# Last-row items: one turned by TensorE again, v's loads reordered, and softmaxes moved ahead of copies on ScalarE

## The chip, the cores and the metric

The kernel runs on one core of a Trainium2 chip. The metric is the device time of one execution in microseconds: 1477.64 before the change (median of three runs, 1477.17 to 1479.41). The engines are called PE (TensorE, matmuls; PEld are its weight loads), ACT (ScalarE), DVE (VectorE), POOL (GpSimd) and SP (SyncE, which here only issues DMAs).

## The reference

```python
# top-k attention, q, k, v: (8, 8, 576, 64) float32
scores = scale * np.matmul(q, k.transpose(0, 1, 3, 2))
kth = np.partition(scores, -top_k, axis=-1)[..., -top_k:-top_k + 1]   # top_k = 32
scores = np.where(scores >= kth, scores, -1e9)
attn = np.exp(scores - np.max(scores, axis=-1, keepdims=True))
attn = attn / (np.sum(attn, axis=-1, keepdims=True) + 1e-09)
x = np.matmul(attn, v)                 # to (4608, 512): tokens by heads * 64
# block with exact gelu
h = x @ w_in                           # (512, 2048)
g = 0.5 * h * (1.0 + erf(h / sqrt(2)))
out = g @ w_out                        # (2048, 512)
```

All arithmetic is in float32.

## The kernel before

**Items and slots.** Two heads of a batch make a pair, so a batch has 4 pairs. 576 query rows are four blocks of 128 and a rest of 64. An *item* is 128 query rows of one pair (both heads, 2 x 576 scores for each row in the tile `s`), or, for the rest, the last 64 rows of two pairs together: a *last-row item* (`items[i][1] == NM`). A batch has 16 ordinary and 2 last-row items; the last-row items stand at the end of an even batch and at the beginning of an odd one. So in each two batches (36 items, `RINGS`) four last-row items stand in a row: 16, 17, 18, 19 and then 52 to 55, 88 to 91, 124 to 127. There are N = 144 items.

The main loop (line 1174) has one *slot* n for each item. It is written out by hand and sets the order of every engine's instructions, in slot n:

- scores of item n+2 on PE (in an even slot those of n+3 too), and ACT's copies of them to `s`, scaled;
- the selection of the 32nd largest score of item n on DVE (`top_k`), with POOL's help (`sum_up`, `smaller`). Its threshold goes from POOL (`threshold`, L516, L517) to ACT;
- the softmax of item n-1 on ACT, for each of the two heads e a `select` (L536, which pushes all scores below the threshold far down) and an exponential (L548) whose sum goes to `den`. POOL adds a small number (`add_small`, L529), DVE takes the reciprocal at the end of its `top_k` (`inverse`, L523), POOL multiplies (`normalise`, L571);
- the transposition of item n-2, which brings keys to the partitions for the product with v. It goes one of two ways. By PE (`transposes`): one transpose of the ends (`tails`, tile `tp_t`, L647) and eight of the main keys (tile `tp`, L661), each followed by ACT's copy to `pt` (L650, L676). Or by DVE and DRAM, where `squared(i)` holds: DVE transposes 32 x 32 squares (`square_p`, L595, in the middle of `top_k`), SP writes the tile to DRAM (`write_p`, `turned`, L605, four DMAs), and a slot later reads it back (`read_p`, L615, four DMAs) into `pt`. Before the change these are all last-row items from 52 on and most even ordinary items;
- the product with v (`attend`, L727 for two ordinary items of a pair at once, L738 for a last-row item) and the copy of the result to `xT` (`copy_x`, L732, L744). There is one `pt` tile for two items. After a pair's last product the next batch's v is loaded into the same buffers (`load("v", ...)`, L138 and L142, four DMAs).

**The block with gelu.** Between all this PE works off a fixed list of pieces (`mlp`): `h_ps` = first product (L790), `gelus` on ACT (L806), and the second product by seven smaller products (L944, L946), whose sums POOL makes (`run_small`, up to six steps a slot). The gelu and the exponential lie in different table sets of ACT, so an odd slot, in which gelus run, has two table loads.

**Banks.** From slot 13 on the short tiles of PE's results (`o`, `t_ps`, `tp_t`, `seven`) all live in one bank with one buffer (`bank`, tag `z`): the next one can be written once ACT has copied the one before. `tp` and one of the two score tiles share the tag `pr`, `h_ps` and the other the tag `l1`.

**Last-row items from 52 on** (`delayed`): their products come later than others. Item 52's stands in slot 56 (`even_last`), those of 53 in the middle of slot 57 and of 54 and 55 in slot 59 (`mid`, `mids`). Each `mids` copies x, issues the next read (`read_p`) and one of the loads of v (`soon`); the others of these loads are kept until the slot's end (`issue`, `late_issues`, `flush`). SP takes all its DMAs in the order of the program, with a wait of one holding those behind it.

Of the kernel before, what the change touches and what calls it, by code (L numbers as in the profile page):

```python
# [14 lines left out]
def kernel(  # L15
# [78 lines left out]
            return raws[n][pair % 2 if pair < SQUARES else 0]  # L94
        return raws[n][pair % len(raws[n])]

    held, late_issues, soon = [False], [], []

    def issue_soon():
        while soon:  # L100
# [9 lines left out]
    def flush():  # L110
        held[0] = False
        while late_issues:
            late_issues.pop(0)()

    def load(n, pair, queue=None, queue2=None):
        if pair >= n_pairs:
# [161 lines left out]
    def bank(name):  # L278

        tag = "z" if few[0] else ("z", "y0", "y1", "y2")[turn[0] % 4]  # L280
        turn[0] += 1
        return ps.tile([P, 512], f32, tag=tag, bufs=1, name=name)
# [292 lines left out]
    def squared(i):  # L575

        if not SINGLE.stop - 2 < i < N - 2:
            return False
        return items[i][1] == NM or (i % 2 == 0 and i % RINGS != 12)

    def delayed(i):

# [117 lines left out]

    copies = []

    def column(tok):

        at = tok % RING
        return at if at < COLS else at - COLS

    def attend(i):

        if i < 0 or i >= N:  # L710
            return False
        pair, t = items[i]
        b, at = divmod(pair, NP)
        if t < NM and t % 2 == 0:
            return False
        pt = pt_now[0]
        o = bank("o")
        n, row = (2 * P, (t - 1) * P) if t < NM else (TL, SM)
        tok = place_of(b, row)
        gap = RING if t == NM else COLS if tok % RING >= COLS else RING - COLS  # L720
        assert read[0] >= tok - gap + n
        c = slice(column(tok), column(tok) + n)
        if t < NM:
            vt = raw_of("v", pair)
            for j in range(NJ):
                for e in range(2):
                    nc.tensor.matmul(  # L727
                        o[e * D : (e + 1) * D, 0:n], lhsT=vt[:, j, e, :],
                        rhs=pt[:, e * NJ + j if j < NM else NM, :],
                        start=(j == 0), stop=(j == NJ - 1),  # L730
                    )
            copies.append(lambda: nc.scalar.copy(out=xT[:, at, c], in_=o[:, 0:n]))  # L732
        else:
            for r in range(2):
                vt = raw_of("v", pair + r)
                for j in range(NJ):
                    for e in range(2):
                        nc.tensor.matmul(  # L738
                            o[e * D : (e + 1) * D, r * TL : (r + 1) * TL],
                            lhsT=vt[:, j, e, :],  # L740
                            rhs=pt[:, e * NJ + j if j < NM else NM, i % 2 * P :][:, half(r, e)],
                            start=(j == 0), stop=(j == NJ - 1),
                        )
            copies.append(lambda: nc.scalar.copy(  # L744
                out=xT[:, at : at + 2, c],
                in_=o[:, 0 : 2 * TL].rearrange("p (r n) -> p r n", n=TL),
            ))

        if t == (NM if b % 2 == 0 else NM - 1):
            for r in range(2 if t == NM else 1):  # L750
                f = lambda r=r: load("v", pair + r + NP)
                if r == 0 and delayed(i):
                    soon.append(f)
                else:
                    issue(f)
        if at == (NP - 1 if t < NM else NP - 2):
            assert n_tok[0] == tok
            n_tok[0] = tok + n
        return True
# [414 lines left out]
    for n in range(ahead):  # L1174

        held[0] = n < N and squared(n - 2)
        mid = [i for i in (n - 5, n - 4) if delayed(i) and n % 2 and (i % 2 or i in starts)]
        even_last = delayed(n - 4) and n % 2 == 0 and n - 4 not in starts
        if not mid and not even_last:
            read_p(n - 3)  # L1180

        def mids():
            attend(mid.pop(0))
            if not mid:
                copy_x()
                read_p(n - 3)
                issue_soon()
        left[0] = room_in(n)
        few[0] = n > START + 2
        eager[0] = n > N  # L1190
        left[0] += closes(n - 3) - closes(n - 2)
        if not waits(unit_in(n)):
            weights_add(unit_in(n))
        if n > 0:
            larger(n + 1)
        for piece in squares_in.pop(n, []):
            piece()
        if n == 1:

            for e in range(2):  # L1200
                select(0, e)
            for e in range(2):
                softmax(0, e)
        two = few[0] and n % 2 == 0 and n + 3 < N and items[n + 3][1] < NM
        scores(n + 2, two)
        if two:
            scores(n + 3)
        if even_last:
            product = attend(n - 4)
            issue_soon()  # L1210
            read_p(n - 3)
        else:
            product = not delayed(n - 3) and attend(n - 3)
        if len(mid) == 2:
            mids()
        late = n > START
        if n != 1 and n < START:

            for e in range(2):
                select(n - 1, e)  # L1220
            softmax(n - 1, 0)
        copy_x()
        if n == START:

            for e in range(2):
                select(n - 1, e)
            softmax(n - 1, 0)
        if waits(unit_in(n)):
            weights_size(unit_in(n))
            weights_add(unit_in(n))  # L1230
        mlp(1)
        if closes(n - 3):
            ready[0] = n_tok[0]
        if few[0] and n % 2:
            run_gelus()
        tr = transposes(n - 2)
        if product and n > START and done[0] < len(pieces) and pieces[done[0]][0] > ready[0]:

            for piece in tr[:1]:
                piece(n + 2 if few[0] else None)  # L1240
            tr, ready[0] = tr[1:], n_tok[0]
        if not few[0] and n > START:
            softmax(n - 1, 0)
        mlp(1)
        if n != 1 and not late:
            softmax(n - 1, 1)
        if few[0]:
            softmax(n - 1, 0)
            if n % 2:
                mlp(ODD)  # L1250
                if mid:
                    mids()
        mlp(1)
        prep = prep_in.pop(n, [])
        if n == 0:
            weights_size(unit_in(1))
            keep_busy(14, ident)
        if n == START + 1:

            for piece in prep:  # L1260
                piece(None)
            prep = []
        if len(prep) > 1 and len(tr) == 3:
            tr, prep = tr[:1] + prep[:1] + tr[1:], prep[1:]
        now = tr[:-1]
        if few[0]:
            now, tr, prep = tr + prep[:1], [], prep[1:]
        for x, piece in enumerate(now):
            piece(n + 2 if few[0] else None)
            ready[0] = n_tok[0]  # L1270
            if few[0] and x == 2:
                break
            mlp(1)
        ready[0] = n_tok[0]
        if late:
            softmax(n - 1, 1)
        if n > 0:
            smaller(n + 1)
        add_small(n - 1)
        for piece in tr[-1:] + prep:  # L1280
            piece(None)
            mlp(1)
        if n < START:

            keep_busy(4 if n == 0 else 8 if product else 14 if n < 5 else 18, ident)

        run_gelus()
        mlp(left[0])
        run_gelus()
        if n < N:  # L1290
            top_k(n, lambda: inverse(n - 1), lambda: square_p(n - 2))
            write_p(n - 2)
            flush()
            if n == 0:
                larger(1)
        else:
            inverse(n - 1)
        threshold(n)
        if n == 0:
            smaller(1)  # L1300
        normalise(n - 1)
        sum_up(n + 2)
        if n in sums_in:
            weight_sums(sums_in[n])
        run_small(6)

        if n > 0 and not waits(unit_in(n + 1)):
            weights_size(unit_in(n + 1))
        run_stores()
        if n == N:  # L1310
            run_stores()
        for m in (n + 1, n + 2):

            if m > 2 and waits(unit_in(m)) == (m == n + 1):
                load_weights(m)
        if n < NP:
            load("v", n)
        if n == 5:
            nc.vector.memset(flat["k"][0][TL:, 0:TL], 0.0)
            load("q", SQUARES)  # L1320
            load("k", SQUARES)
# [38 lines left out]
```

## Time and profile before

| | us |
|---|---|
| median of 3 runs (lowest to highest) | 1477.64 (1477.17 to 1479.41) |
| the profiled execution, its own time | 1479.29 |
| span of that execution, first to last instruction | 1477.5 |
| busy: PE | 1449.7 (98%) |
| busy: DVE | 1307.8 (89%) |
| busy: POOL | 1142.0 (77%) |
| busy: ACT | 1082.8 (73%) |
| mean granted clock of PE | 0.999 |

A row of the timeline gives the start and the duration in microseconds, the engine, the line, the operation, the written and the read tiles, shapes and a count; the brackets give the idle time of the engine before it and what ended that. PE's records are halves of a matmul: x12 are six matmuls. "SPq" rows are the issues of DMAs on SP's queue. A row of the waits names who waited, for whom, the total, how often and the longest. A row of a group gives the busy time and the mean length of one, then the idle time before.

### The profile page before, as it was taken

Reading aid. Unit: us, or ns where it says so; the run is one execution under the profiler, and the core shown is the slowest. Engines: PE = TensorE matmul, PEld = TensorE weight load, DVE = VectorE, ACT = ScalarE, POOL = GpSimd, SP = SyncE. Lnnn points to the kernel's source line nnn. Section 1 sums busy time; section 2 is a strip of 40 time slices with the busy share of each in tenths; the row PEclk is TensorE's granted clock in tenths of the full one; section 3 lists DMA queues with packets and bytes.
Section 4 is the critical chain, followed back from the end, with each engine's and each line's share of the span. In section 5 each row is a group of like instructions: output and inputs, shape, how many; then the busy total and the mean of one; then the engine's idle time right before and its main releaser. Section 6 shows DMA issues by size and latency. Waiting matters only on the chain. (4 is left out here: it accounts for less than half of the span.)

```text
span 1477.5 us, 26521 instructions
## 1 busy us (share of the span) xinstructions
PE 1449.7 (98%) x8693; PEld 1134.6 (77%) x8693; DVE 1307.8 (89%) x3331; ACT 1082.8 (73%) x1902; POOL 1142.0 (77%) x1290
## 2 busy tenths in 40 slices
PE   8999999999999998999999999999999999999999
PEld 6776677887777776888777777787777777787787
DVE  7999899999999999899999999899999999898701
ACT  7999877877777686777777777677777777677620
POOL 6877567878898888777898978787788888887632
PEclk9999999999999999999999999999999999999999
DMA  7425210045435356345534347344543435523300
GB/s 198 144 86 129 78 47 1 24 92 103 93 71 91 67 107 129 65 95 112 102 81 78 74 74 151 76 92 96 99 101 73 89 63 97 125 61 73 68 15 15
DMA packets 544713, 127.04 MB, mean 86 GB/s; under 512 B 466464, under 2 KB 536128, under 8 KB 544576
## 3 DMA queue, kind: packets, MB, share of 16 engines
q1 hardware_dynamic: 543312, 124.93, 39.8%
q8 instruction: 69, 1.13, 0.3%
q14 instruction: 68, 0.56, 0.1%
q10 hardware_dynamic: 1200, 0.39, 0.1%
q0 software_dynamic: 64, 0.03, 0.0%
HBM read 80.47 MB, written 44.83 MB: 85 GB/s over the span
## 5 line engine op out<-in xcount | busy, mean ns | idle before, releaser
L790 PE MATMUL h_ps<-xT,w_in_sb 128*128 128x256 f32 (+1 forms) x2560 | 534.1, 361 | 0.0
L790 PEld LDWEIGHTS h_ps<-xT,w_in_sb 128*128 128x128 f32 x2560 | 437.5, 190 | 73.3 <-issue 25.2
L502 DVE MAX8 top<-lists 128x8 f32<-128x576 f32 (+1 forms) x792 | 475.5, 639 | 0.0
L505 DVE MATCH_REPLACE8 lists<-top,lists 128x288 f32<-128x288 f32 (+1 forms) x528 | 307.6, 588 | 0.0
L571 POOL TENSOR_TENSOR s<-s,stat 128x1152 f32<-128x1152 f32 x135 | 286.1, 2119 | 0.3 <-DVE stat L523 0.3
L536 ACT ACTIVATE s<-s,stat 128x576 f32<-128x576 f32 x288 | 224.7, 788 | 16.6 <-POOL stat L516 16.4
L548 ACT ACTIVATE s<-s,stat 128x576 f32<-128x576 f32 x288 | 224.6, 782 | 11.3 <-POOL lists L466 0.7
L529 POOL TENSOR_SCALAR stat<-stat 128x2 f32<-128x2 f32 x144 | 31.6, 219 | 210.4 <-ACT s L548 183.8
L474 POOL TENSOR_TENSOR lists<-lists 128x576 int32<-128x576 int32 x132 | 186.4, 1412 | 4.0
L466 POOL TENSOR_TENSOR lists<-s 128x576 int32<-128x576 int32 x133 | 188.0, 1413 | 0.0
L727 PE MATMUL o<-pt,raw_v 128*64 128x256 f32 x1280 | 152.9, 384 | 4.3 <-DMA pt<-turned 2.4
L806 ACT ACTIVATE g<-h_ps 128x512 f32<-128x512 f32 x144 | 78.2, 594 | 107.0 <-PE h_ps L790 106.8
L727 PEld LDWEIGHTS o<-pt,raw_v 128*64 128x64 f32 x1280 | 87.9, 136 | 88.3 <-issue 43.1
L946 PE MATMUL y_ps<-w_out_sb,sum 128*128 128x256 f32 x472 | 140.8, 380 | 0.0
L414 ACT ACTIVATE s<-s_ps 128x1024 f32<-128x1024 f32 x127 | 124.9, 1031 | 9.2 <-PE s_ps L406 8.8
L406 PE MATMUL s_ps<-kt,qm 64*128 64x512 f32 x512 | 129.4, 618 | 0.8 <-ACT s L412 0.8
L676 ACT COPY pt<-tp 128x1024 f32<-128x1024 f32 x73 | 74.4, 1019 | 56.2 <-PE tp L661 56.1
L505 DVE MATCH_REPLACE8 lists<-first,lists 128x288 f32<-128x288 f32 x264 | 114.2, 438 | 0.0
L946 PE MATMUL y_ps<-w_out_sb,g 128*128 128x256 f32 x480 | 113.4, 379 | 0.0
L523 DVE RECIPROCAL stat<-stat 128x2 f32<-128x2 f32 x144 | 22.9, 159 | 95.2 <-POOL stat L529 94.4
L502 DVE MAX8 first<-lists 128x8 f32<-128x288 f32 x268 | 106.5, 436 | 0.0
L441 DVE TENSOR_TENSOR lists<-s 128x576 f32<-128x576 f32 x133 | 101.1, 760 | 0.0
(162 smaller groups left out, 2483.3 us busy)
## 6 DMA issues: line engine op xcount, KB each, us to landing
turned<-s SPq DMA_DIRECT2D x240, 144.0 KB, 3.5
pt<-turned SPq DMA_DIRECT2D x240, 144.0 KB, 3.2
raw_v<-in_v_dram SPq DMA_DIRECT2D x64, 128.0 KB, 3.0
raw_q<-in_q_dram SPq DMA_DIRECT2D x112, 72.0 KB, 2.3
raw_k<-in_k_dram SPq DMA_DIRECT2D x112, 72.0 KB, 2.4
out_dram<-y SPq DMA_DIRECT2D x30, 256.0 KB, 2.1
w_out_sb<-in_moe_w_in_dram SPq DMA_DIRECT2D x14, 511.8 KB, 4.8
w_out_sb<-in_moe_w_out_dram SPq DMA_DIRECT2D x10, 511.8 KB, 4.1
```

What stands on the lines that cost most here:

```text
L406: nc.tensor.matmul(s_ps[:, e], lhsT=q_t[rows, :], rhs=kt[rows, main_keys(pair)], start=True, stop=True)
L414: nc.scalar.activation(spread(s, S + TL, SM), s_ps, func=AF.Copy, scale=scale)
L466: nc.gpsimd.tensor_tensor(t[:, :, 1].bitcast(i32), a.bitcast(i32), b.bitcast(i32), op=ALU.add)
L474: nc.gpsimd.tensor_tensor(into_of(i)[:, :, 1].bitcast(i32), both, top, op=ALU.subtract)
L502: nc.vector.max(x[:, e], src[:, e])
L505: nc.vector.match_replace(dst[:, e], x[:, e], src[:, e], LOWEST)
L536: nc.scalar.activation(s, s, func=AF.Prelu, bias=st["neg"][:, e : e + 1], scale=1.0, alpha=STEEP)
L548: nc.scalar.activation(s, s, func=AF.Exp, bias=st["bias"][:, e : e + 1], scale=1.0, accum_out=st["den"][:, e : e + 1],)
L571: nc.gpsimd.tensor_tensor(s, s, wide, op=ALU.mult)
L727: nc.tensor.matmul(o[e * D : (e + 1) * D, 0:n], lhsT=vt[:, j, e, :], rhs=pt[:, e * NJ + j if j < NM else NM, :], start=(j == 0), stop=(j = ...
L790: nc.tensor.matmul(h_tile(u)[:, i, :], lhsT=w_in_sb[:, ko, f * P : (f + 1) * P], rhs=xT[:, ko, c0 : c0 + n], start=(ko == 0), stop=(ko == ...
L946: nc.tensor.matmul(acc[names][:, k], lhsT=lhsT, rhs=rhs, start=(j == 0 and k == 0), stop=(j == FT // 2 - 1 and k == 1),)
```

## The change

It has three parts.

1. `squared` no longer holds for item 17 of each 36 (i % RINGS == RINGS // 2 - 1). From 52 on that is items 53, 89 and 125, the second last-row item of an even batch: it is transposed by PE in slot i + 2. Its product comes in slot i + 3 right behind that of the item before, both in one bank (`shared`, offset `off`) with one copy to `xT` of four times 64 columns. So slot 57 has no product in its middle, and the read of item 54 stands at its beginning.
2. The loads of v are issued in the order of the pairs: both of the delayed item's go through `soon`, now first in first out, one of the next item's to the end of the slot, the other (`later`) to the end of the slot after. The stores of y at the end of slot 57 move behind the read at the beginning of slot 58 (`stores_later`; the same 36 and 72 slots on).
3. From slot 20 on, `ahead_of_x`: in every even slot, and in odd slots but those with n % 36 from 15 to 23, the softmax of item n-1 is moved forward on ACT. In an even slot: select 0, exponential 0, select 1, then the copy of x, then exponential 1 (before: the copy, select 0, exponential 0, ... and select 1, exponential 1 after the copies of the transposes). In an odd slot: both selects, then the gelus, the copy of `seven`, and both exponentials, then the copies of the transposes (before: gelus, copy of `seven`, select 0, exponential 0, copies of the transposes, select 1, exponential 1).

In the built program POOL's order is the same. PE has the nine transposes more for each of the three items and their products moved forward, DVE has the three transposes less, SP the write and the read of the three items less and the new order of the loads, and ACT the copies of the transposes more, one copy of x less, and the new order of the softmaxes.

```diff
@@ load queue helpers
-    held, late_issues, soon = [False], [], []
+    held, late_issues, soon, later = [False], [], [], []
...
         while late_issues:
             late_issues.pop(0)()
+        late_issues.extend(later)
+        later.clear()
@@ def squared(i)
-        return items[i][1] == NM or (i % 2 == 0 and i % RINGS != 12)
+        if items[i][1] == NM:
+            return i % RINGS != RINGS // 2 - 1
+        return i % 2 == 0 and i % RINGS != 12
@@ def attend(i)
-        o = bank("o")
+        both = t == NM and delayed(i - 1) and not delayed(i)
+        alone = t < NM or not delayed(i) or delayed(i ^ 1)
+        o = shared.pop() if both else bank("o")
+        off = 2 * TL if both else 0
...
-                            o[e * D : (e + 1) * D, r * TL : (r + 1) * TL],
+                            o[e * D : (e + 1) * D, off + r * TL : off + (r + 1) * TL],
...
-            copies.append(lambda: nc.scalar.copy(
-                out=xT[:, at : at + 2, c],
-                in_=o[:, 0 : 2 * TL].rearrange("p (r n) -> p r n", n=TL),
-            ))
+            if not alone:
+                shared.append(o)
+            else:
+                first = 0 if both else at
+                copies.append(lambda: nc.scalar.copy(
+                    out=xT[:, first : at + 2, c],
+                    in_=o[:, 0 : off + 2 * TL].rearrange("p (r n) -> p r n", n=TL),
+                ))
...
-                if r == 0 and delayed(i):
-                    soon.append(f)
+                if delayed(i):
+                    soon.insert(0, f)
+                elif both and r:
+                    later.append(f)
                 else:
                     issue(f)
@@ the main loop
+        def stores_later(m):
+            return m % 2 == 0 and delayed(m - 3) and m - 4 in starts
+
         even_last = delayed(n - 4) and n % 2 == 0 and n - 4 not in starts
-        if not mid and not even_last:
+        if not mid:
             read_p(n - 3)
+        if stores_later(n):
+            run_stores()
...
+        few[0] = n > START + 2
+        ahead_of_x = few[0] and n > RINGS // 2 and (n % 2 == 0 or not -4 < n % RINGS - RINGS // 2 < 6)
         left[0] = room_in(n)
-        few[0] = n > START + 2
...
             product = attend(n - 4)
+            attend(n - 3)
             issue_soon()
-            read_p(n - 3)
...
+        if ahead_of_x:
+            select(n - 1, 0)
+            if n % 2 == 0:
+                softmax(n - 1, 0)
+            select(n - 1, 1)
         copy_x()
+        if ahead_of_x and n % 2 == 0:
+            softmax(n - 1, 1)
...
         if few[0]:
-            softmax(n - 1, 0)
+            if n % 2 or not ahead_of_x:
+                softmax(n - 1, 0)
             if n % 2:
+                if ahead_of_x:
+                    softmax(n - 1, 1)
                 mlp(ODD)
...
-        if late:
+        if late and not ahead_of_x:
             softmax(n - 1, 1)
...
-        run_stores()
+        if not stores_later(n + 1):
+            run_stores()
```

More of the change, by code (lines that the diff above doesn't have):

```diff
@@ L701 @@
     copies = []
+    shared = []
     def column(tok):
```

## The prediction

> **What bounds the kernel now.** I read the page first, then who waited for whom on TensorE (PE), then busy time in three stretches, then single slots in order of time. The page's first section:
>
> ```profile
> PE 1449.7 (98%) x8693; PEld 1134.6 (77%) x8693; DVE 1307.8 (89%) x3331; ACT 1082.8 (73%) x1902; POOL 1142.0 (77%) x1290
> ```
>
> PE works through one fixed order and is idle for 1477.5 - 1449.7 = 27.8 us, start and end included. Time can be won only from those idle stretches, and work added to PE costs its full length. Who PE waited for (us in total, times, longest):
>
> ```profile
> PE o L738 <- DMA pt<-turned: 5.7, 3, 2.2
> ...
> PE o L727 <- DMA pt<-turned: 2.4, 2, 1.9
> PE t_ps L371 <- ACT xT L744: 2.2, 3, 0.7
> ...
> PE tp_t L647 <- POOL s L571: 1.5, 4, 0.5
> ...
> PE o L727 <- ACT s L548: 1.2, 1, 1.2
> ```
>
> The first three are the last-row items. They sit in slots 56 to 60 and the two repeats 36 slots on, and come to 5.7 + 2.4 + 2.2 = 10.3 us; here they are in stretches (busy time of PE, PEld, DVE, ACT, POOL), beside eight ordinary slots:
>
> ```profile
> 545.00:565.00 20.00, 19.26 (x156) 15.36 (x153) 18.89 (x47) 14.21 (x25) 19.34 (x23) 1.00 0.72 149
> 565.00:592.00 27.00, 23.74 (x190) 18.59 (x189) 24.72 (x67) 16.27 (x29) 22.66 (x27) 1.00 0.57 122
> ...
> 692.00:768.00 76.00, 76.00 (x409) 59.61 (x409) 71.29 (x185) 57.44 (x103) 64.68 (x73) 1.00 0.47 95
> ```
>
> In the ordinary slots PE is never idle: 76 us for eight slots is 9.5 each. DVE needs 71.29 / 8 = 8.9, so it can gain on PE by up to 0.6 us a slot if nothing holds it.
>
> **The change part by part.** *PE work added.* Items 53, 89 and 125 (the second last-row item of an even batch) are turned by PE again: one transpose of the ends and eight of the main keys each.
>
> ```profile
> 579.73 0.27 PE L647 MATMUL tp_t<-ident,s 128*128 128x128 f32 x1
> 579.84 0.60 PE L946 MATMUL y_ps<-w_sum,sum 128*128 128x256 f32 x2
> ...
> 580.71 1.04 PE L661 MATMUL tp<-ident,s 128*128 128x128 f32 x8
> 581.58 0.60 PE L946 MATMUL y_ps<-w_sum,g 128*128 128x256 f32 x2
> ```
>
> From start to next start that is 0.11 + 0.87 = 0.98 us an item, 2.9 us for three, in a full PE stream: **+2.9**. [...]
>
> ```profile
> L661 PE MATMUL tp<-ident,s 128*128 128x128 f32 x600 | 77.9, 273 | 0.0
> ```
>
> Also gone: three DVE transposes of 1.36 us (row at 559.60 below) and, from SP's queue, four writes and four reads of each item. Added on ACT: two copies an item (0.27 and 1.01 us), less one of two xT copies; ACT is 73% busy, so they count only where PE waits for ACT in that slot. I take nothing.
>
> *The wait for the xT copy.* The copy at 558.89 followed a second `attend` in the middle of slot 57. Both products now stand together in slot 56, an even slot, in one bank with one copy. There six matmuls lie between the product and the next user of the bank (704.83 to 707.38 in the even slot shown below, 2.5 us), which cover the copy: the 2.2 us go.
>
> ```profile
> 559.19 0.49 PE L371 MATMUL t_ps<-kt,qm 128*128 128x128 f32 x2 [0.74 <-ACT xT L744]
> ```
>
> *The waits for the read-back.* The page's row for a write to DRAM, DVE's transposes of items 55 and 56, then SP's queue:
>
> ```profile
> turned<-s SPq DMA_DIRECT2D x240, 144.0 KB, 3.5
> ```
>
> ```profile
> 559.60 1.36 DVE L595 STREAM_TRANSPOSE s<-s 128x1152 f32<-128x1152 f32 x1
> ...
> 569.86 1.36 DVE L595 STREAM_TRANSPOSE s<-s 128x1152 f32<-128x1152 f32 x1
> ```
>
> ```profile
> 558.10 3.15 SPq L615 DMA_DIRECT2D pt<-turned  x4
> ...
> 563.76 3.27 SPq L605 DMA_DIRECT2D turned<-s  x4
> 567.08 0.99 SPq L138 DMA_DIRECT2D raw_v<-in_v_dram  x1
> ...
> 571.48 2.60 SPq L615 DMA_DIRECT2D pt<-turned  x4
> 574.19 3.39 SPq L605 DMA_DIRECT2D turned<-s  x4
> ```
>
> Item 55 was turned by 560.96 but written from 563.76, 2.8 us late, behind the read of item 54 and a load of v. Its own read then stood behind the next load of v and the store of y. In the new order the first of these loads comes before the read at 558.10, the second still between item 55's write and its read, the store behind the read. The write can start about 561.3, when the read of item 54 is issued, is issued by 564.6 and lands 3.5 us later (the page's median for such a write), at 568.1: the read goes out some 3.4 us earlier. PE arrives 0.74 us earlier, without the xT wait, and 0.98 us later from the transposes in slot 55, so a wait of at most 2.2 us goes with over 1 us to spare. Item 56's write follows at about 571.5 instead of 574.19, 2.7 us earlier, while PE comes up to 0.74 + 2.2 - 0.98 = 2.0 us earlier; its waits (2.4 us in two rings) fall to about 0.5. The three lines together: **-9.8** (bounds: -2.2, if the reads stay as late, and -10.3).
>
> *ACT's new order.* In an even slot both selects and one exponential now stand ahead of the xT copy:
>
> ```profile
> 701.63 1.94 ACT L414 ACTIVATE s<-s_ps 128x1024 f32<-128x1024 f32 x2 [0.21 <-PE s_ps L406]
> ...
> 704.83 0.37 ACT L732 COPY xT<-o 128x256 f32<-128x256 f32 x1 [1.25 <-PE o L727]
> 705.10 0.78 ACT L536 ACTIVATE s<-s,stat 128x576 f32<-128x576 f32 x1
> ...
> 705.96 0.78 ACT L548 ACTIVATE s<-s,stat 128x576 f32<-128x576 f32 x1
> ...
> 707.38 0.38 PE L371 MATMUL t_ps<-kt,qm 128*128 128x128 f32 x2
> ```
>
> From 703.57, select, exponential with its read, and select take 2.5 us, the copy 0.37: done at 706.4, and PE needs its bank at 707.38. It is free here, with 0.9 us over; where a threshold comes late it may miss by a few tenths: **+0.5** (bounds 0 and 0.9 in each of a few slots, 3).
>
> In an odd slot two selects now stand ahead of the gelus, and a select waits for POOL's threshold:
>
> ```profile
> 730.73 0.79 POOL L516 TENSOR_SCALAR stat<-top 128x2 f32<-128x2 f32 x1 [0.60 <-DVE stat L523]
> 730.93 1.09 ACT L806 ACTIVATE g<-h_ps 128x512 f32<-128x512 f32 x2 [2.04 <-PE h_ps L790]
> ...
> 731.90 0.38 ACT L965 COPY p<-seven 128x256 f32<-128x256 f32 x1
> ...
> 732.15 0.80 ACT L536 ACTIVATE s<-s,stat 128x576 f32<-128x576 f32 x1
> ...
> 733.01 1.28 ACT L548 ACT_TABLE_LOAD   x1
> ...
> 734.18 0.38 PE L371 MATMUL tp_t<-kt,qm 128*128 128x128 f32 x2
> ...
> 736.45 1.06 ACT L676 COPY pt<-tp 128x1024 f32<-128x1024 f32 x1
> ...
> 738.07 1.99 PE L406 MATMUL s_ps<-kt,qm 64*128 64x512 f32 x8
> ```
>
> The threshold is there at 731.52. Two selects (1.6) and a table load (1.28) put the gelus at 734.4 instead of 730.93, 3.5 us late. The copy of `p` (bank of tp_t) would then end at 735.8, 1.6 us after PE wants the bank, and the pt copy at 741.0; the second score pair, 0.96 us into the scores, needs that bank at 739.0. So with DVE where it is now the first such slot costs PE 2.0 us. But a stalled PE lets DVE gain those 2.0 us, and from then on thresholds come earlier: with both exponentials done sooner, DVE no longer has to wait for their sums, which it does now:
>
> ```profile
> DVE stat L523 <- POOL stat L529: 94.4, 91, 9.8
> ```
>
> So it is an entry price, paid where the odd slots of the new kind begin: slots 25, 61, 97 and 133. I take 0.8 us at each, since DVE brings part of the lead: **+3.2** (bounds 0 and 4 x 2.0 = 8). The lead should also cure the waits for POOL's product (late thresholds) and part of the last wait: **-1.8** (bounds 0 and -2.7).
>
> **Sum:** 2.9 - 9.8 + 0.5 + 3.2 - 1.8 = -5.0 us. The profiled execution took 1479.29 (span 1477.5, 1.8 around it), 1.65 above the median of the runs shown; this gives 1474.3 for it and **1472.6** for the median.
>
> **Rivals.** *Better:* DVE brings the whole lead and nothing is paid at the entries: 2.9 - 10.3 - 2.7 = -10.1, so 1467.5. For it speak the 94.4 us that DVE waits; against it, at 730.73 POOL itself waited for DVE, which had nothing to spare in that slot.
>
> *Traded, no change:* the read-back waits go, but they were what let DVE catch up; full price at all four entries, late thresholds in even slots: 2.9 - 9.8 + 8 + 1.5 = +2.6, 1480.2; with half of the -1.8 still won, 1479.3. For it: in slots 56 to 60 PE was idle for 0.74 + 3.26 us by the two stretches above, and DVE could come nearer in that time.
>
> *Slower:* DVE loses its lead again and again, and the gelus wait behind the selects. POOL carries the threshold, and in slots with six small sums its own round is longer than PE's 9.5:
>
> ```profile
> 555.43 0.22 POOL L529 TENSOR_SCALAR stat<-stat 128x2 f32<-128x2 f32 x1
> ...
> 565.69 0.22 POOL L529 TENSOR_SCALAR stat<-stat 128x2 f32<-128x2 f32 x1
> ```
>
> That is 10.26 us. If two such slots in a row eat 1.5 us of lead three times a ring, ten times in all, it adds 15 - 3.2: +6.8, 1484.4. It decides once the threshold comes later than 1.5 us before h_ps ends. [...]
>
> ```profile
> L536 ACT ACTIVATE s<-s,stat 128x576 f32<-128x576 f32 x288 | 224.7, 788 | 16.6 <-POOL stat L516 16.4
> ```
>
> Against the slower case: over eight ordinary slots POOL needs 64.68 of 76 us.
>
> *Not what it says:* the reads stay as late, since the DMA engines are busy here (their share of the first stretch above is 0.72): 2.9 - 2.2 + 0.5 + 3.2 - 1.8 = +2.6, 1480.2.
>
> **How the numbers follow.** Forecast 0.48, better 0.14, traded 0.20, slower 0.10, not what it says 0.08. What a measurement can tell from no change is 0.2%, 3 us: 1474.7 to 1480.6. The forecast's own range is 1469 to 1476; 0.04 of it is within the bound, as are 0.17 of traded and 0.05 of the last case. Faster 0.58, same 0.26, slower 0.16. The range that leaves out the slower case and the end of the better one is 1467.5 to 1481.
>
> **What would show it.** Right: no PE wait on pt<-turned over 0.5 us; none on the xT copy behind L738; DVE's wait for POOL's sums far below 94.4; an added PE stall of about a microsecond in slots 25, 61, 97, 133 and none between. Wrong: PE waiting for ACT's pt or p copy in many odd slots, gelus that follow the threshold by 3 us instead of h_ps, or the read of item 55 still landing after PE has arrived.

## The result and the profile after

The changed kernel took 1472.78 us in the median of six runs (1472.55 to 1473.40), the kernel before 1477.8 beside it (1477.17 to 1479.41): ratio 0.9964, interval 0.9952 to 0.9975, below 1 by more than the 0.2% that count as no change. The profiled execution's own time is 1472.55, its span 1470.8, 6.7 us less than before. The forecast was 1472.6. That the total fits so well is in part luck: the terms for the xT copy and for the odd slots came out otherwise by 2 to 3 us each, in opposite directions.

The page's first section after the change (busy time of each engine):

```profile
PE 1451.4 (99%) x8720; PEld 1135.5 (77%) x8720; DVE 1312.2 (89%) x3328; ACT 1070.4 (73%) x1905; POOL 1137.7 (77%) x1290
```

PE is busy 1.7 us longer and idle 1470.8 - 1451.4 = 19.4 us instead of 27.8. Who PE waits for now (us in total, times, longest):

```profile
PE tp_t L373 <- ACT xT L757: 3.0, 3, 1.0
...
PE tp_t L373 <- ACT p L980: 1.5, 4, 0.4
...
PE o L736 <- DMA pt<-turned: 0.5, 1, 0.5
```

The waits for the read-back, 5.7 + 2.4 before, are down to 0.5. The waits for POOL's product (1.5) and for the exponential (1.2) have gone. Two rows are new: 3.0 for a copy of xT, one microsecond in each of three rings, and 1.5 for the copy of `p`. DVE's wait for POOL's sums, a sign that the prediction named, fell from 94.4:

```profile
DVE stat L525 <- POOL stat L531: 74.8, 74, 6.2
```

The two stretches around slots 55 to 60 (their length, busy time of PE, PEld, DVE, ACT, POOL, then PE's clock):

```profile
545.00:565.00 20.00, 20.00 (x163) 15.80 (x160) 18.24 (x46) 15.35 (x28) 19.01 (x24) 1.00 0.58 116
565.00:592.00 27.00, 26.00 (x202) 20.44 (x201) 25.32 (x67) 17.86 (x33) 23.14 (x27) 1.00 0.52 115
```

PE's idle time in them falls from 0.74 and 3.26 to 0 and 1.00. SP's queue in that place:

```profile
558.92 2.57 SPq L619 DMA_DIRECT2D pt<-turned  x4
561.93 3.52 SPq L609 DMA_DIRECT2D turned<-s  x4
...
568.85 2.58 SPq L619 DMA_DIRECT2D pt<-turned  x4
...
572.65 4.57 SPq L609 DMA_DIRECT2D turned<-s  x4
```

Item 55 is written at 561.93 instead of 563.76 and read at 568.85 instead of 571.48, so its product at 575.83 waits for nothing. The new wait comes right behind that product, in slot 59:

```profile
575.82 0.22 POOL L518 TENSOR_SCALAR stat<-top 128x2 f32<-128x2 f32 x1 [0.56 <-DVE stat L525]
...
575.83 1.39 PE L747 MATMUL o<-pt,raw_v 128*64 128x64 f32 x40
...
576.08 0.78 ACT L538 ACTIVATE s<-s,stat 128x576 f32<-128x576 f32 x1 [0.82 <-POOL stat L518]
576.92 1.28 ACT L550 ACT_TABLE_LOAD   x1
...
578.99 0.24 ACT L757 COPY xT<-o 128x128 f32<-128x128 f32 x1
...
579.28 0.49 PE L373 MATMUL tp_t<-kt,qm 128*128 128x128 f32 x2 [1.00 <-ACT xT L757]
```

The product ends at 577.2, but ACT copies it only at 578.99. A select, a table load and an exponential stand ahead of the copy, and the select waited for POOL's threshold. PE's next short tile needs the same bank.

The kernel before had one more loss, in the third ring, that the prediction did not see:

```profile
1271.00:1274.00 3.00, 0.80 (x17) 0.53 (x17) 3.00 (x10) 2.03 (x2) 2.92 (x3) 0.98 0.92 188
1274.00:1277.00 3.00, 3.00 (x35) 2.61 (x32) 3.00 (x11) 1.16 (x4) 2.86 (x3) 0.50 0.71 111
1277.00:1280.00 3.00, 3.00 (x20) 2.76 (x19) 2.04 (x3) 0.91 (x3) 0.00 (x0) 0.95 0.35 102
```

```profile
1266.27 1.39 PE L738 MATMUL o<-pt,raw_v 128*64 128x64 f32 x40
...
1273.51 2.12 PE L738 MATMUL o<-pt,raw_v 128*64 128x64 f32 x40 [2.20 <-DMA pt<-turned]
```

After PE's wait of 2.20 us for the read of the ring's fourth last-row item (127, as item 55 is in the first ring) the granted clock was 0.50, and the same product took 2.12 us instead of 1.39. The clock's loss over these nine microseconds is 3 x 0.02 + 3 x 0.50 + 3 x 0.05 = 1.7 us. It shows on no list of waits, since PE counts as busy. In the changed kernel the longest wait in these slots is 1.0 us, and its mean clock is 1.000 instead of 0.999.

### The profile page after: what moved, and what is told of

It is laid out like the page before. It is cut to its first block, busy times and chain, and to the rows that moved or that the text cites. A ratio compares the mean times of both kernels' runs of the same rounds, so it can differ in the third digit from the quotient of the medians.

```text
span 1470.8 us, 26630 instructions
## 1 busy us (share of the span) xinstructions
PE 1451.4 (99%) x8720; PEld 1135.5 (77%) x8720; DVE 1312.2 (89%) x3328; ACT 1070.4 (73%) x1905; POOL 1137.7 (77%) x1290
## 5 line engine op out<-in xcount | busy, mean ns | idle before, releaser
L538 ACT ACTIVATE s<-s,stat 128x576 f32<-128x576 f32 x288 | 218.1, 781 | 106.5 <-POOL stat L518 106.4
L550 ACT ACTIVATE s<-s,stat 128x576 f32<-128x576 f32 x288 | 224.2, 782 | 7.3
L443 DVE TENSOR_TENSOR lists<-s 128x576 f32<-128x576 f32 x133 | 108.8, 818 | 4.2 <-ACT s L381 2.1
L680 ACT COPY pt<-tp 128x1024 f32<-128x1024 f32 x76 | 77.6, 1021 | 39.0 <-PE tp L665 38.9
L961 PEld LDWEIGHTS y_ps<-w_out_sb,g 128*128 128x128 f32 x480 | 91.2, 190 | 12.4
```

The costliest lines, as they stand in the source:

```text
L538: nc.scalar.activation(s, s, func=AF.Prelu, bias=st["neg"][:, e : e + 1], scale=1.0, alpha=STEEP)
L550: nc.scalar.activation(s, s, func=AF.Exp, bias=st["bias"][:, e : e + 1], scale=1.0, accum_out=st["den"][:, e : e + 1],)
L961: nc.tensor.matmul(acc[names][:, k], lhsT=lhsT, rhs=rhs, start=(j == 0 and k == 0), stop=(j == FT // 2 - 1 and k == 1),)
```

## The experiments

Each ratio is to the kernel before, run beside it. There the kernel before took 1479.2 to 1480.6 in the median, more than the 1477.8 beside the first result, so ratios are compared first. The changed kernel itself took 1472.78 and, measured again, 1473.01.

**Parts 1 and 2 alone, part 3 alone.**

```diff
-        ahead_of_x = few[0] and n > RINGS // 2 and (n % 2 == 0 or not -4 < n % RINGS - RINGS // 2 < 6)
+        ahead_of_x = False
```

> ACT's old order, with the item turned by PE and the new order of SP's queue. Theory T (the read-back waits carry the gain, ACT's order is worth little by itself): read-back waits 5.7 + 2.4 and the xT wait 2.2 gone, 2.9 added by the transposes; DVE still waits some 90 us for POOL's sums; the 1.5 us behind POOL's product and the 1.2 us behind the exponential stay. 1471 to 1474. Rival R (DVE's lead, which ACT's order brings, is what makes the last-row items timely): reads still late by 1 to 2 us a ring, 1477 or more.

Measured: 1474.79, ratio 0.9965 (0.9951 to 0.9979). That is 0.8 us above theory T's range, beside a kernel before that took 1479.98, and the xT wait did not go. For part 3 alone, that line and the code that it governs went into the kernel before.

> The kernel before with ACT's new order alone. Theory T: the read-back waits stay (SP's order sets them) and grow a little since PE arrives earlier or as early; the waits behind POOL's product and the exponential (2.7) fall, some waits behind ACT's copies come: 1475.5 to 1478. Rival R: DVE is ahead by some 2 us, so items 55 and 56 are turned and read earlier and the read-back waits fall by more than half: 1473 or less.

Measured: 1479.03, ratio 0.9991 (0.9982 to 1.0000). So parts 1 and 2 carry the gain, and part 3 is worth little by itself; the rival's lead of DVE is there (its wait for POOL's sums falls to 75.0), but it does not make the reads timely. The waits of PE in these two, parts 1 and 2 first:

```profile
PE tp_t L373 <- ACT xT L757: 4.7, 3, 1.6
...
PE o L736 <- DMA pt<-turned: 0.6, 1, 0.6
```

```profile
PE o L738 <- DMA pt<-turned: 4.3, 2, 2.5
...
PE o L727 <- DMA pt<-turned: 3.9, 2, 2.0
```

The wait for the xT copy in slot 59 is there without part 3, and longer. So ACT's new order did not make it. A late read had covered it: in the kernel before the product of that slot itself waited, 1.21 us at 576.82 in the first ring.

**The turn without the queue's new order, and the order without the turn.** Both have part 3, so the run with part 3 alone is their base. First the item turned by PE, with the old rule for loads and stores:

```diff
-                if delayed(i):
-                    soon.insert(0, f)
-                elif both and r:
-                    later.append(f)
+                if r == 0 and delayed(i):
+                    soon.append(f)
...
-            return m % 2 == 0 and delayed(m - 3) and m - 4 in starts
+            return False
```

> The changed kernel, with v's loads and the stores back in the old order on SP's queue. Theory T (the order of the queue cures the read of item 55): the write of item 55 is late again behind a load, PE waits 1 to 2 us for its read in each of three rings: 1475 to 1478. Rival (that item 53 no longer goes over DRAM is enough): no such wait over 0.5 us, within 0.7 us of the changed kernel's 1472.8.

Measured: 1480.37, ratio 1.0004 (0.9995 to 1.0013): the whole gain is gone. In seven of its eleven runs the mean clock was 0.997 or less; these took 1481.18 in the median, the three with 1.000 took 1478.67, so part of the loss goes with the clock. The profiled execution (1480.37, mean clock 0.999) had a clock of 0.52 over 1277 to 1280, behind a wait of PE of 3.16 us. Its SP queue:

```profile
556.04 0.66 SPq L140 DMA_DIRECT2D raw_v<-in_v_dram  x1
...
563.32 0.48 SPq L144 DMA_DIRECT2D raw_v<-in_v_dram  x1
563.86 2.57 SPq L619 DMA_DIRECT2D pt<-turned  x4
...
573.62 2.54 SPq L619 DMA_DIRECT2D pt<-turned  x4
```

Since the products of items 52 and 53 now stand in one slot, the old rule lets three loads go (556.04 to 563.8) before the read of item 54, which is 4.9 us later than with the new rule; item 55 is read at 573.62. PE waited 2.85 us for it:

```profile
578.99 1.39 PE L747 MATMUL o<-pt,raw_v 128*64 128x64 f32 x40 [2.85 <-DMA pt<-turned]
```

Then the new order with items 53, 89 and 125 over DRAM as before:

```diff
-            return i % RINGS != RINGS // 2 - 1
+            return True
...
-                if delayed(i):
+                if delayed(i) and i % RINGS != RINGS // 2 - 1:
                     soon.insert(0, f)
...
-        if not mid:
+        if not mid and not even_last:
             read_p(n - 3)
...
-            attend(n - 3)
             issue_soon()
+            read_p(n - 3)
```

> ACT's new order and the changed order of SP's queue, but items 53, 89 and 125 go over DVE and DRAM as before; it differs from the run with ACT's order alone only on SP: both loads for item 52's pairs stand ahead of the read of item 54, those for item 53's pairs behind the write of item 55, the stores behind the read of item 55. Theory T (the order of the queue is what made the reads timely, the turn by PE is worth only the xT wait it removes): read-back waits below 2 us in all, the xT wait of 2 us stays, 2.9 us of transposes saved: 1472 to 1474. Rival (SP's queue has no room for the write and the read of item 53 as well): the read-back waits stay at 5 to 8 us, 1476 or more.

Measured: 1486.18, ratio 1.0054 (1.0040 to 1.0067). My theory fell, and the loss is larger than its rival said: PE's waits for the read-back are 7.9 + 6.4 = 14.3 us instead of 5 to 8, and the mean clock was 0.995 to 0.998. Two loads here stand ahead of the read of item 53 and the write of item 54, and everything behind comes later:

```profile
552.36 2.57 SPq L619 DMA_DIRECT2D pt<-turned  x4
...
563.12 2.53 SPq L619 DMA_DIRECT2D pt<-turned  x4
...
574.60 2.57 SPq L619 DMA_DIRECT2D pt<-turned  x4
```

Item 54 is read at 563.12 and item 55 at 574.60, 5.7 us later than with the turn. So neither part does anything good by itself: 0.9991 with neither, 1.0004 and 1.0054 with one, 0.9950 with both (the changed kernel's second measurement, below). The turn takes a write (3.5 us) and a read (2.6) off SP's queue, and the order decides whether the reads or the loads get that room. Not all of the room is work: here the queue issued nothing for 4.6 us between the end of item 54's write (555.04 + 3.46 = 558.50) and its read. In the kernel before, where reads waited 71 times for a write to land, 108.1 us in all, four transfers of v went out in that time (554.52 to 557.6).

**The stores alone put back** ahead of the read of item 55, the loads as changed.

```diff
-            return m % 2 == 0 and delayed(m - 3) and m - 4 in starts
+            return False
```

> The changed kernel with the stores of y ahead of the read of item 55 again (1.0 to 2.2 us on SP's queue), all else as changed. Theory (the loads' order carries the gain of part 2): the read is issued up to 2 us later than 568.9 and lands at 574.6 to 576.6, PE wants it at 575.8: 0 to 1 us per ring, 1473 to 1475. Rival (the store is as bad as the loads): a wait of 2 us or more in each ring, with the half clock that followed such a wait in the kernel before, 1478 or more.

Measured: 1472.55, ratio 0.9949 (0.9935 to 0.9962), like the changed kernel. The read went out at 569.98 instead of 568.85, and its product still waited for nothing; in the second ring it waited 0.36. The loads' order is what counts in part 2.

**The changed kernel again, and part 3 in even or odd slots alone.**

> The changed kernel once more, on the chip of the runs beside it, so that they can be compared with it: a ratio to the kernel before of 0.9952 to 0.9975, as in its first runs.

Measured: 1473.01, ratio 0.9950 (0.9938 to 0.9963).

```diff
+        ahead_of_x = few[0] and n > RINGS // 2 and n % 2 == 0
```

> ACT's new order in the even slots alone, with the item turned by PE and the new queue. Theory T: DVE's lead comes from here, since both sums of an even slot are ready sooner; its wait for POOL's sums falls from 92.7 to below 80, PE's wait for POOL's product (1.6) stays or falls a little, and no waits for the copy of p come, as gelus stay ahead of the selects: 1 to 2 us below parts 1 and 2 alone. Rival: the even slots bring nothing, the odd ones do: within 0.5 us of parts 1 and 2 alone.

Measured: 1473.43, ratio 0.9952 (0.9938 to 0.9966), like the changed kernel's and 1.9 us by the ratios below parts 1 and 2 alone, though the two intervals overlap.

```diff
+        ahead_of_x = few[0] and n > RINGS // 2 and n % 2 == 1 and not -4 < n % RINGS - RINGS // 2 < 6
```

> ACT's new order in the odd slots alone (without those near the last-row items), with the item turned by PE and the new queue. Theory T: selects ahead of the gelus wait for POOL's threshold without DVE's lead from the even slots, so the stalls that the forecast called an entry price (0.8 each, up to 2.0) show: 1 to 3 us above parts 1 and 2 alone. Rival: PE's buffers absorb the late gelus here too: within 1 us of parts 1 and 2 alone, or below.

Measured: 1477.64, ratio 0.9983 (0.9974 to 0.9992), against 0.9965 without part 3. So the odd slots alone cost about 2.7 us (the difference of the ratios, 0.0018, of 1480; the intervals just overlap, but the spans of the two profiles, 1476.0 and 1472.6, say 3.4), as theory T said. Together with the even slots they cost nothing in sum: 1473.01 against 1473.43. PE's waits for the copy of `p`, odd slots alone:

```profile
PE tp_t L373 <- ACT p L980: 4.3, 7, 1.0
```

Slot 25 shows why, first with the odd slots alone, then in the changed kernel:

```profile
246.80 0.22 POOL L518 TENSOR_SCALAR stat<-top 128x2 f32<-128x2 f32 x1
...
247.05 1.44 ACT L538 ACTIVATE s<-s,stat 128x576 f32<-128x576 f32 x2 [0.64 <-POOL stat L518]
...
250.11 0.59 PE L961 MATMUL y_ps<-w_out_sb,sum 128*128 128x256 f32 x2
...
250.77 0.38 ACT L980 COPY p<-seven 128x256 f32<-128x256 f32 x1
...
251.21 0.49 PE L373 MATMUL tp_t<-kt,qm 128*128 128x128 f32 x2 [0.50 <-ACT p L980]
```

```profile
245.94 0.22 POOL L518 TENSOR_SCALAR stat<-top 128x2 f32<-128x2 f32 x1 [0.30 <-DVE stat L525]
...
246.19 1.44 ACT L538 ACTIVATE s<-s,stat 128x576 f32<-128x576 f32 x2 [1.84 <-POOL stat L518]
...
249.61 0.59 PE L961 MATMUL y_ps<-w_out_sb,sum 128*128 128x256 f32 x2
...
249.92 0.38 ACT L980 COPY p<-seven 128x256 f32<-128x256 f32 x1
...
250.35 0.49 PE L373 MATMUL tp_t<-kt,qm 128*128 128x128 f32 x2
```

In both the copy of `p` ends about 4.4 us behind the threshold's start. With the even slots' order the threshold comes 0.86 us earlier; PE itself stands 0.50 earlier in that profile (249.61 against 250.11), so 0.36 of it is a lead. From the start of the matmul before to the start of the one that needs the bank it is 1.10 us with the odd slots alone and 0.74 in the changed kernel, against 0.43 (249.94 to 250.37) without part 3. So the lead takes about half of this slot's price away. The even slots' gain was expected to show in DVE's wait for POOL's sums too, below 80; it fell from 92.7 only to 87.6, so that part of the reasoning was too bold. With the odd slots alone it is 94.1, with both 74.8.

**Part 3 in all odd slots,** those near the last-row items too.

```diff
+        ahead_of_x = few[0] and n > RINGS // 2
```

> The changed kernel, with ACT's new order also in the odd slots 15 to 23 of each 36, which the change leaves out. Theory T: there the last-row items and four more short products stand close, PE waits sooner for ACT's copies, and POOL's threshold comes latest: 0.5 to 3 us slower than the changed kernel, with waits for the copies of p and pt in slots 51 to 59. Rival: no difference over 0.5 us.

Measured: 1482.78, ratio 1.0028 (1.0017 to 1.0038), some 0.8% more than the changed kernel's and far over what I expected. Part of it is the clock: all seven runs have a mean of 0.996 to 0.998. In the slot of the last product ACT holds two selects for POOL's threshold, behind them the xT copy, and PE needs the bank at once:

```profile
574.49 0.22 POOL L518 TENSOR_SCALAR stat<-top 128x2 f32<-128x2 f32 x1 [0.56 <-DVE stat L525]
...
574.74 1.44 ACT L538 ACTIVATE s<-s,stat 128x576 f32<-128x576 f32 x2 [5.93 <-POOL stat L518]
...
576.09 0.24 ACT L757 COPY xT<-o 128x128 f32<-128x128 f32 x1
...
576.47 1.10 PE L959 MATMUL seven<-w_sum,g 128*128 128x256 f32 x4 [2.35 <-ACT xT L757]
```

In the list of waits this is 7.2 us in three rings, and 3.7 more for `p` where other short products follow. After the wait of 2.35 us shown here the clock was 0.93 over 576 to 578, 0.50 over 578 to 580 and 0.72 over 580 to 582, another 1.7 us.

**The transposes' price.**

```diff
-                turn_over(tp[:, e], e)
+                for _ in range(2 if i > SINGLE.stop and i % RINGS in (7, 9, 11) else 1):
+                    turn_over(tp[:, e], e)
```

> The changed kernel with the eight transposes of the main keys made twice in nine ordinary items (43, 45, 47 and the same 36 and 72 later), 72 transposes more with the same result. [...]

Two estimates from the trace of the kernel before: by the distance of the starts, 0.98 us for nine or 109 ns each, 72 transposes cost 7.8 us; by the mean length of one, 273 ns, 19.7 us.

Measured: 1480.86, ratio 1.0012 (1.0003 to 1.0021). Its span is 1479.3, against 1471.5 for the changed kernel's second profile: 7.8 us more, 108 ns for each of 72. The ratios, 1.0012 and 0.9950, would give 9.2 us, but they carry the spread of the kernel before; the two times compared here have a mean clock of 1.000. The groups of transposes in that second profile and in this one say 88.9 - 81.0 = 7.9, 110 ns each:

```profile
L665 PE MATMUL tp<-ident,s 128*128 128x128 f32 x624 | 81.0, 273 | 0.0
```

```profile
L665 PE MATMUL tp<-ident,s 128*128 128x128 f32 x696 | 88.9, 273 | 0.0
```

The mean length, 273 ns, is not what a further transpose costs.

**The new wait taken away.** In slots 59, 95 and 131 ACT copies x ahead of the softmax:

```diff
+            if mid:
+                mlp(ODD)
+                mids()
+                softmax(n - 1, 0)
+            else:
...
```

> The changed kernel, but in slots 59, 95 and 131 (product of item 55 in the middle) ACT copies x ahead of the select of item n-1, head 0, which waits there for POOL's threshold. Theory T: the new wait of PE for the xT copy (3.0 us in three rings) goes and nothing takes its place: 1469.5 to 1470.5. Rival: PE runs into the next limit in the same slot or the next one (the read of item 56, the copy of p), the wait only moves: 1472 to 1473.

Measured: 1472.16, ratio 0.9946 (0.9933 to 0.9958), about the changed kernel's. The rival was right: the wait for the xT copy (3.0) has gone, and PE waits 3.7 us for the next read instead.

```profile
PE o L736 <- DMA pt<-turned: 3.7, 3, 1.5
```

```profile
571.80 1.01 SPq L876 DMA_DIRECT2D out_dram<-y  x2
572.92 5.03 SPq L609 DMA_DIRECT2D turned<-s  x4
580.75 2.54 SPq L619 DMA_DIRECT2D pt<-turned  x4
```

DVE had turned item 56 by 571.8, but the stores stood ahead of its write. So the stores went behind it:

```diff
-        if stores_later(n):
-            run_stores()
...
             flush()
+            if stores_later(n):
+                run_stores()
```

> Copy first, as above, and the stores of y that stood ahead of the write of item 56 now behind it. With the copy first PE waited 3.7 us in three rings for the read of item 56, whose write began 1.1 us after DVE had turned it, behind the stores (1.01 us). Theory: read and write come 1.1 us earlier in each ring and the wait falls from 3.7 to about 0.5: 3 us less than the changed kernel, a ratio near 0.9945. Rival: the write is slow for another reason or the next limit shows at once, no more than 1 us won, ratio 0.996.

Measured: 1470.74 (1470.50 to 1470.98), ratio 0.9934 (0.9922 to 0.9947), beside the changed kernel's 1473.01 (1472.47 to 1474.21): 2.3 us less, where 3 were expected, and faster than both kernels.

```profile
571.64 3.37 SPq L609 DMA_DIRECT2D turned<-s  x4
...
579.08 2.54 SPq L619 DMA_DIRECT2D pt<-turned  x4
```

```profile
PE o L736 <- DMA pt<-turned: 1.8, 2, 1.2
```

The write starts 1.3 us and the read 1.7 us earlier. Half of the 3.7 is left, in the second and third ring.

## Why the prediction was right, and where it was not

The total was right: 1472.6 forecast, 1472.78 measured; for the profiled execution -5.0 forecast and 1472.55 - 1479.29 = -6.7 measured. That is in part luck, since a cost that it missed (the xT copy) and a price that it set too high (the odd slots) nearly cancel. By its terms:

| term | forecast | by the profile or a run |
|---|---|---|
| 27 transposes | +2.9 | +2.9 (108 to 110 ns each in the run with 72 more) |
| read-back waits | -7.6 (8.1 to 0.5) | -7.6 (8.1 to 0.5; 1.7 left in the second profile) |
| xT copy | -2.2 | +0.8 (2.2 gone, 3.0 in slot 59) |
| odd slots' entry | +3.2 | +0.3 by the list of waits (about 1.0 by PE's starts) |
| late thresholds | -1.8 | -1.4 (2.7 gone, 1.3 of it now a wait for `p`) |
| even slots | +0.5 | no cost seen |
| half clock | not seen | -1.7 |

The right column gives -6.7, as measured; with 1.0 for the odd slots it gives -6.0, so the fit to a tenth means nothing.

*Transposes:* right, and measured by themselves.

*Read-back:* right in size and nearly in time (write forecast at 561.3, seen at 561.93; read 3.4 us earlier, seen 2.6; item 56's write forecast at 571.5, seen at 572.65 behind the stores). But the prediction took the turn as a mere price and gave the gain to the order of the queue. The runs show that the order without the turn is slower than before, and the turn without the order is worth nothing, so the size holds only for both together. The step that failed is "also gone ... from SP's queue, four writes and four reads", which was given no value.

*xT copy:* the wait behind the product of item 53 went as said. The step that failed is that nothing took its place. Item 55's product now started on time, and ACT was the next to be late, with the old order as well (4.7 in the run of parts 1 and 2). The prediction asked what is late next for SP, not for ACT in the same slot.

*Odd slots:* the mechanism, gelus behind a waiting select and a late copy of `p`, is there and costs 2.7 us when the odd slots are moved alone, near the +3.2. With the even slots moved too it is there but mis-sized. Of the four entries the list of waits shows only slot 61, with 0.26; by PE's starts, against the run of parts 1 and 2 alone, slots 25, 61 and 97 lose 0.30, 0.42 and 0.25. The better case ("DVE brings the whole lead") came true for most of the price, not for all. The other three waits for `p`, 1.26 in all, at 424.7 and its like, stand where PE had waited for POOL's product before: one late threshold, another engine to be named.

*Late thresholds:* the 1.5 for POOL's product and the 1.2 for the exponential went, but with the even slots alone they are still there (1.5 and 1.7), and with the odd slots alone they are gone. The prediction put this down to DVE's lead, while the runs give it to the odd slots' order, and 1.3 of it only changed its name.

*Slower rival:* it needed DVE to lose its lead again and again. That did not happen in the slots that the change touches, where no wait for `p` is over 0.43. In those that it leaves out, two selects held by the threshold cost 0.8%, by a nearer way: the xT copy behind them (PE waited 2.35 us for it), and the clock of 0.50 after it.

*Not what it says:* did not happen for the reads.

## What to carry to other kernels

When a wait is taken away, follow the same slot engine by engine for what is late next: here a read had covered a copy, the copy a read behind a store, and the changed kernel with both further edits took 1470.7. (The stores moved without the copy were not run.) In a queue that runs in program order, room and order are one thing; test them together, as either alone gained nothing (1.0004 and 1.0054). Ahead of an instruction that others need soon, do not put one that waits for another engine, unless the wait is known to be over by then: selects that stood 5.93 us behind the threshold held the xT copy for which PE waited 2.35.

## What the runs showed of the hardware

A pause of PE cost more than its length in some cases. In the run with the new order but without the turn, PE stood idle for three microseconds waiting for the read of item 55 (3.19 us in all), and the clock was 0.57 over the next three (columns as in the stretches above):

```profile
577.00:580.00 3.00, 0.00 (x0) 0.00 (x0) 3.00 (x11) 2.80 (x4) 3.00 (x3) 1.00 0.89 269
580.00:583.00 3.00, 2.95 (x42) 2.78 (x43) 3.00 (x9) 0.27 (x1) 2.30 (x2) 0.57 0.89 162
```

The kernel before had it after a wait of 2.20 us (shown above). It did not follow every such pause: after the 2.85 us quoted from the run with the old rule of the queue the clock was 1.00 over 578 to 588, and the same product took 1.39 us. The changed kernel and the run of parts 1 and 2 alone, whose longest waits behind a read or a copy in these slots are 1.0 and 1.6 us, have a mean clock of 1.000. Here 2.20 was enough once, and 2.85 not.

All profiles together say the same, from slot 20 to the last items: there are twelve waits of PE of 2.20 to 3.19 us, six with a half clock (0.50) behind them (2.20, 2.35, 2.45, 2.48, 3.16, 3.19) and six without (2.25, 2.32, 2.34, 2.36, 2.47, 2.85), and none behind the shorter ones whose clock was read, of up to 1.98. Each of the six stretches lost 1.7 us of clock. So the length alone does not decide; what else does is not shown.

The kernel before spreads from 1476.6 to 1482.7 us in all its runs, the changed one only from 1472.5 to 1474.2, and that goes with the clock. Of the 62 runs of the kernel before beside the experiments, 20 have a mean clock of 1.000 and a median of 1478.3 us, and 26 have 0.998 or less and a median of 1480.85; all eleven runs of the changed kernel have 1.000. No run changed the clock alone, so its share of the gain is not shown apart.
